# An attention-and-feed-forward kernel: its front in another order, plain v loaded sooner and without a block-diagonal copy

## Chip, cores and metric

The kernel runs on one core of a Trainium2 chip. Times are device microseconds of one execution. Engines are called PE (TensorE, matrix products), DVE (VectorE), ACT (ScalarE), POOL (GpSimd) and SP (SyncE, which here only issues DMAs). POOL, SP and ACT issue DMAs; a load that casts from float32 to float16 on its way is issued by POOL.

## What is computed

The attention of 8 batches with 8 heads of 576 positions and 64 dimensions feeds a gated feed-forward block. Four heads see a plain window of 32 positions, four a dilated one (every fourth of 128). Cut to what matters:

```
mask_plain = (rel >= 0) & (rel < 32)
mask_dil = (rel >= 0) & (rel < 128) & (rel % 4 == 0)
attn = softmax(where(mask, q @ k.T / 8, -1e9))       # heads 0-3 plain, 4-7 dilated
x = (attn @ v).transpose(0, 2, 1, 3).reshape(4608, 512)
out = (gelu(x @ w_gate) * (x @ w_val)) @ w_out       # 512 -> 1536 -> 512
```

## The kernel before

**Tiles.** A unit of attention is a pair of heads of one batch, numbered n: n // 4 is the batch, and for batch 0 n = 0 and 1 are plain pairs and 2 and 3 dilated ones. The results of pair n go to a quarter of x transposed, `xT[pair(n)]`, 128 rows by 4608 tokens. The feed-forward block runs in 9 chunks of 512 tokens. Each chunk has 12 blocks nb of 128 hidden units; a block takes a gate and a value product of four 512-wide matmuls each (line 611, one for each quarter kc of x), then ACT's gelu (g) and DVE's multiply (u). The second product, line 618, follows.

**Words.** The order of the work is written out by hand in strings of words (`gate_words`, `out_words`), one word after another, read by `run_program`. A number counts feed-forward matmuls taken from a list in the order that `orders` gives (block, gate or value, quarter). The others name a unit: c casts loaded q or k to float16, t turns it with PE transposes (t0 to t3 plain, t4 to t7 dilated; q and k of each pair) and copies it out of PSUM, b puts mask biases into PSUM, S makes scores, P the exponential (ACT), D the sums of exponentials, N the product with v, and X (DVE) the division into xT. The reciprocal of a sum comes either from T and B on DVE (two 32x32 transposes and a reciprocal), or from A, which is l and r on ACT (a logarithm and an exponential). W is a filler product on ones; G loads ACT's gelu table; V issues the next loads.

**The front.** Chunk 0 can't start before the attention of batch 0, so the string for c == 0 (lines 802 to 805) does that first: this is "the front". Ahead of it, lines 674 to 698 issue loads and warming products. SP loads q of the plain heads in two halves (line 676), ACT k likewise. `gate["dma"]` holds a DMA that the next gated load must wait for; here the loop leaves the second half of q in it, and the first plain v load (line 235, `load_v(0, 0, True)`, four loads of 144 KB into `stage`) waits for that. POOL issues the dilated q and k (`load_eights`, line 176, four loads), six casting loads of dilated v (lines 301 and 309), then the first two pairs of gate and value weights (`load_w`, line 153), then casts plain v into `vdiag` (`cast_diag`, line 255), then the third pair of weights. [...]

**Plain v of batch 0.** `vdiag` is block-diagonal: the two heads of a pair lie in opposite corners of a 128x128 block, with zeros (line 195, on DVE) in the other two, so that N of a plain pair of batch 0 is 10 full-size matmuls (line 435). All other N units are pairs of 64x64 tiles (line 446), two matmuls for each block.

Of the kernel before, what the change touches and what calls it, by code (L numbers as in the profile page):

```python
# [9 lines left out]
F16 = mybir.dt.float16  # L10
F32 = mybir.dt.float32
# [10 lines left out]
def kernel(  # L22
# [10 lines left out]
    nc = tc.nc  # L33
    B, H, S, D = q.shape
    NT, DM = out.shape
    DFF = moe_w_gate.shape[1]
    P = 128
    NHP = H // 2
# [13 lines left out]
    NB2 = S // BK  # L52
# [5 lines left out]
    const = ctx.enter_context(tc.tile_pool(name="const", bufs=1))  # L58
# [22 lines left out]
    xT = [const.tile([P, NT], F16, tag=f"xT{i}", name=f"xT{i}") for i in range(NKC)]  # L81

    vraw = [const.tile([P, 4 * NB2 * D], F16, tag=f"v{i}", name=f"v{i}") for i in range(3)]
    vdiag = const.tile([P, 2 * NB2 * P], F16, tag="vdiag")
    qraw = [const.tile([P, 2 * QK], F16, tag=f"q{i}", name=f"q{i}") for i in range(2)]
    stage = const.tile([P, 3840], F32, tag="stage")
    s16 = const.tile([P, 4608], F16, tag="s16")
# [52 lines left out]
    def biases():  # L140
        for x in range(2):
            half = slice(64 * x, 64 * x + 64)
            nc.vector.tensor_scalar(bias[half, 0:BQ], band[half, 64 * x : 64 * x + BQ], 1.0, BIG, ALU.subtract, ALU.mult)
        rest = bias[:, BQ : BQ + BK]
        rest_mask(nc.vector, rest)
        nc.vector.tensor_scalar(rest, rest, 1.0, BIG, ALU.subtract, ALU.mult)

    def load_w(*parts):

        for i in parts:  # L150
            for t, w in ((wg_t, moe_w_gate), (wv_t, moe_w_val)):
                src = w[:, WC[i][0] : WC[i][1]].rearrange("(kc p) n -> p kc n", p=P)
                nc.gpsimd.dma_start(out=t[i], in_=src)
# [7 lines left out]
    gate = {}  # L161
# [6 lines left out]
    def rows_in(src, r):  # L168

        return src.rearrange("h (p r) d -> p h (r d)", r=r)  # L170
# [15 lines left out]
    def at2(t, c0, dims):  # L186
        base = t[:, c0 : c0 + 1]
        return bass.AP(tensor=base.tensor, offset=base.offset, ap=[base.ap[0]] + dims)

    diag = vdiag.rearrange("p (e c) -> p e c", c=P)  # L190

    def zero():

        for x in range(2):
            nc.vector.memset(at2(vdiag[64 * x : 64 * x + 64].bitcast(F32), 32 - 32 * x, [[64, 2 * NB2], [1, 32]]), 0.0)

    def st_of(i):
        return stage[:, 1280 * i : 1280 * i + 1280]

# [28 lines left out]
    def load_v(b, i, plain):  # L228

        st = st_of(i)  # L230
        for g in range(2 * plain):
            for x in range(2):
                rows_ = v[b, 2 * g + x].rearrange("(j p) d -> p j d", p=64)
                dst = st[half_of(x, b and g), 576 * g : 576 * g + 576].rearrange("p (j d) -> p j d", j=NB2)
                gated(nc.sync.dma_start(out=dst, in_=rows_))
        for g in range(2 - 2 * plain):
            for x in range(2):
                half = st[half_of(x, g), 576 * g : 576 * g + 512]
                rows_ = v[b, HK + 2 * g + x, 0 : 4 * P].rearrange("(i p r) d -> p i (r d)", i=2, r=4)
                nc.sync.dma_start(out=half.rearrange("p (i c) -> p i c", i=2), in_=rows_)  # L240
        for x in range(2 - 2 * plain):
            dst = st[half_of(x), 512:1152].rearrange("p (g c) -> p g c", c=64)[:, 0:10:9]
            heads = slice(HK + 1, HK + 3) if x else slice(HK, HK + 4, 3)
            nc.sync.dma_start(out=dst, in_=v[b, heads, S - 64 : S].rearrange("g p d -> p g d"))
# [2 lines left out]

        nc.gpsimd.tensor_copy(dst, st_of(i)[:, 0:1152].rearrange("p (e d) -> p e d", d=D))  # L248

    def cast_diag(g):  # L250

        st = st_of(0)[:, 0:1152].rearrange("p (e d) -> p e d", d=D)
        at = slice(NB2 * g, NB2 * g + NB2)
        for x in range(2):
            nc.gpsimd.tensor_copy(diag[half_of(x), at, half_of(x)], st[half_of(x), at])

    def half_of(x, swap=0):
        y = x ^ (1 if swap else 0)
        return slice(64 * y, 64 * y + 64)

    def odd(n):

        return n % 2 if n >= NHP else 0
# [72 lines left out]
    def pair(n):  # L336
        return (n + 2 * (n // NHP in (2, 3))) % NHP

    def is_plain(n):
        return pair(n) < NHP // 2  # L340
# [54 lines left out]
    def win(n, at):  # L395

        bank, kind = at // 10, at % 10
        return 512 * bank + ((0, 832, 960, 0) if is_plain(n) else (80, 880, 880, 64))[kind]
# [13 lines left out]
    def bias_first(n, bank):  # L412

        base = base_of(n, bank)
        tiles["bias", n] = True

        def part(c0, step, k, w, src=None, st=False):
            rhs = at2(bias, BQ if src else 0, [[0, k], [1, w]])
            o = at2(psf, base + c0, [[step, k], [1, w]])
            nc.tensor.matmul(o, ident, rhs, start=st, stop=False, skip_group_check=True)  # L420

        if is_plain(n):
            part(0, BQ, 5, BQ, st=True)
            part(5 * BQ, BQ, 3, BQ, st=True)
            part(8 * BQ, BK, 1, BK)
        else:
            part(0, 176, 3, BQ, st=True)
            part(BQ, 176, 2, 80)
            part(2 * 176 + BQ, 176, 2, 80, st=True)
            part(3 * 176, 176, 1, BQ)  # L430
            part(LD - BK, BK, 1, BK, src=True)

    def emit(mms):
        for o, lhs, rhs, st, end in mms:
            nc.tensor.matmul(o, lhs, rhs, start=st, stop=end, skip_group_check=True)

    def emit_tiles(*lists):

        queues, at = [list(mms) for mms, _ in lists], [0.0] * len(lists)
        while any(queues):  # L440
            i = min((i for i in range(len(lists)) if queues[i]), key=lambda i: at[i])
            o, lhs, rhs, st, end = queues[i].pop(0)
            at[i] += max(int(np.prod(rhs.shape[1:])), 72)
            for x in range(2):
                rows, cols = half_of(x), half_of(x, lists[i][1])
                nc.tensor.matmul(o[cols], lhs[rows], rhs[rows], start=st, stop=end, skip_group_check=True)  # L446
# [91 lines left out]
    def two_num_mms(n, i):  # L538
        b, hp = n // NHP, n % 2
        _, _, _, _, vp, vd = tiles["two", b]  # L540
        tiles["num", n] = win(n, i)
        if is_plain(n):
            vp = vp if b else diag
            return two_mms(n, win(n, i), lambda e: vp[:, NB2 * hp + e, :])
        return two_mms(n, win(n, i), lambda e: vd[:, NB2 * hp + (8 if e is None else e % 2 * 4 + e // 2), :])

# [6 lines left out]

    def two_num(n, i):
        mms = two_num_mms(n, i)
        if n < NHP and is_plain(n):
            emit(mms)
        else:
            emit_tiles((mms, odd(n)))

    def two_t(n):
        dt = nrm.tile([P, 18, 32], F32, tag="dt", bufs=1)
# [93 lines left out]
    def warm(n, bank, rows=P, cols=CH):  # L656

        for _ in range(n):
            nc.tensor.matmul(ps[0:rows, bank, 0:cols], ones[:, 0:rows], ones[:, 0:cols], start=True, stop=True)
# [14 lines left out]
    for h in range(0, HK, 2):  # L674
        for t, src, eng in ((0, q, nc.sync), (1, k, nc.scalar)):
            first = eng.dma_start(out=first_p[:, t, h : h + 2], in_=rows_in(src[0, h : h + 2], 6))
            if t == 0:
                gate["dma"] = first
    load_v(0, 0, True)
    nc.scalar.preload_act_table_set("natural_log_exp_and_others")  # L680
    identity()
# [4 lines left out]
    v_cast(0, 1)  # L686
    tiles["two", 0] = views(0)

    warm(69, 7, 32, 32)
    warm(4, 7)  # L690
    nc.vector.tensor_reduce(class_of, ident.rearrange("p (i r) -> p r i", r=4), axis=mybir.AxisListType.X, op=ALU.max)
    biases()
    zero()
    bias_first(0, 4)
    load_w(0, 1)
    for g in range(2):
        cast_diag(g)
    load_w(2)

    def second():  # L700
# [97 lines left out]
    def gate_words(c):  # L798

        if c == 0:  # L800
            return (
                "c0@0 c1@0 t0@0@1 t1@1@0 b1@6 W1@3@0 S0@4 P0 t4@0@1 W1@3@0 c2@0 c3@0 t5@1@0 t2@2@1 t3@3@0 D0@40 T0 B0 "
                "t6@1@1 W10@7 t7@0@0 S1@6 P1 b2@2 S2@2 P2 D1@60 T1 B1 b3@0 S3@0 P3 D2@20 A2 N0@40 X0 D3@00 N2@60 X2 A3 N3@20 1 "
                "N1@00 X1 X3 G V 15 g0 u0 g1 u1 4 g2 4 g3 4 u2 4 u3 4 g4 4 g5 4 u4 4 u5 4 g6 4 g7 4 u6 4 u7 4 g8 4 g9 4 u8 3 "
                "y0@4@5 y1@6@7 1 u9 8 g10 u10 1 t12@4@1 t14@6@0 t13@5@1 t15@7@0 7 g11 u11"
            )
        loads = {1: "F3", 2: "R", 3: "F5 H5", 4: "F6 H6", 5: "F7 H7"}.get(c, "")
        rest = " ".join(f"4 g{nb} 4 u{nb}" for nb in range(2, NNB - 1))
        if c == 1:
            return f"{loads} 8 G 3 g0 1 u0 3 g1 1 u1 {rest} 4 g{NNB - 1} 4"  # L810
        before = f"e3@{c - 1}" if c < NCH - 1 else ""
        return f"{before} {loads} 7 G 3 g0 1 u0 1 g1 4 u1 {rest} 4 g{NNB - 1} 4" + (f" u{NNB - 1}" if c > 6 else "")

    def out_words(c):
# [15 lines left out]
        )  # L830

    orders = {
        0: "000 100 002 102 010 110 012 112 001 101 011 111 003 103 013 113",
        1: "002 003 012 013 000 010 102 103 112 113 001 011 100 110 101 111",
        2: "002 003 000 102 103 100 012 013 010 001 011 101 112 113 110 111",
        3: "000 001 002 100 101 102 010 011 012 003 013 103 110 111 112 113",
# [39 lines left out]
```

## Time and profile before

| | us |
|---|---|
| three runs | 326.84, 327.86, 326.78; median 326.84 |
| profiled execution | 327.72 |
| its span, first to last instruction | 326.0 |
| PE busy | 320.4 (98%) |
| ACT busy | 159.6 |
| DVE busy | 150.3 |
| POOL busy | 82.2 |
| line 611, gate and value products | 112.5 and 112.3 |
| line 618, output products | 96.3 |

The profile is of one execution. An instruction's line there is a line of the kernel before; the timeline merges neighbours of one kind ("x40") and gives start, length, engine, line, operation, tiles, and in brackets the idle time ahead of it and what ended it. [...] stream of 512-wide products, each shown as about 380 ns, starts one every 216 ns. The span has 1.7 us around it in the profiled execution's own time. TensorE's clock is given as fully granted for the whole execution.

### The profile page before, as it was taken

What the parts mean: (1) busy time and instruction counts of PE and PEld (TensorE: products, weight loads), DVE (VectorE), ACT (ScalarE), POOL (GpSimd) and SP (SyncE); (2) the same over time, 40 slices, a digit from 0 to 9 for tenths busy, and PEclk for the clock granted to TensorE, in tenths of its full rate; (3) what the DMA queues carried; (4) which work ended last, traced back from release to release, by engine and by line L of the source; (5) the groups of instructions that cost most, each with busy time, mean ns of one, the idle gap of its engine ahead of it and who ended that gap; (6) DMA issues with size and microseconds to landing.
All of it is one profiled execution on the core that took longest, in us unless ns stands there. A gap on an engine that the chain in (4) does not pass through costs nothing.

```text
span 326.0 us, 7737 instructions
## 1 busy us (share of the span) xinstructions
PE 320.4 (98%) x3207; PEld 156.5 (48%) x3207; DVE 150.3 (46%) x226; ACT 159.6 (49%) x240; POOL 82.2 (25%) x134
## 2 busy tenths in 40 slices
PE   7999999999999999999999999999999999999996
PEld 5854544444444454445444454445444544444443
DVE  6864636444644464346533654456334644204310
ACT  2662567435753556346633763366435753233321
POOL 8875603402473332241133201411000000000000
DMA  8999997998699997897789527973000200020002
GB/s 190 185 198 206 205 187 154 268 177 197 162 279 166 215 206 212 196 227 176 204 207 226 129 101 161 243 173 103 32 2 1 101 33 0 2 97 32 0 34 97
DMA packets 106659, 47.11 MB, mean 144 GB/s; under 512 B 83584, under 2 KB 102144, under 8 KB 106624
## 3 DMA queue, kind: packets, MB, share of 16 engines
q1 hardware_dynamic: 93120, 38.29, 50.2%
q0 software_dynamic: 12944, 7.67, 16.9%
q10 hardware_dynamic: 560, 0.66, 0.7%
q8 instruction: 25, 0.41, 0.5%
q14 instruction: 10, 0.08, 0.1%
HBM read 37.75 MB, written 9.44 MB: 145 GB/s over the span
## 4 chain that ended last, share of the span: by engine, by line
PE 92%; DMA 2%; POOL 2%; ACT 1%; DVE 1%; issue 0%
PE ps L611 57%; PE ps L618 28%; PE ps L446 6%; DMA wg<-in_moe_w_gate_dram 2%; POOL xT L176 1%; PE ps L642 1%; POOL v L301 1%; ACT P L476 0%; DVE P L481 0%; ACT L793 0%; POOL v L309 0%; PE ps L366 0%; PE ps L386 0%; POOL band L117 0%; ACT g L770 0%
## 5 line engine op out<-in xcount | busy, mean ns | idle before, releaser
L775 DVE SCALAR_TENSOR_TENSOR u_all<-g,ps 128x512 f16<-128x512 f16 x108 | 74.1, 687 | 110.1 <-PE ps L611 93.4
L770 ACT ACTIVATE g<-ps 128x512 f16<-128x512 f32 x108 | 63.6, 597 | 104.0 <-PE ps L611 104.0
L611 PE MATMUL ps<-xT,wg 128*128 128x512 f16 x432 | 112.5, 379 | 0.2 <-DMA wg<-in_moe_w_gate_dram 0.2
L611 PE MATMUL ps<-xT,wv 128*128 128x512 f16 x432 | 112.3, 379 | 0.0
L618 PE MATMUL ps<-wo,u_all 128*128 128x512 f16 x420 | 96.3, 380 | 0.0
L611 PEld LDWEIGHTS <-wv 128*128 128x128 f16 x432 | 42.1, 98 | 51.1 <-DMA wv<-in_moe_w_val_dram 0.6
L611 PEld LDWEIGHTS <-wg 128*128 128x128 f16 x432 | 42.2, 98 | 50.6 <-DMA wg<-in_moe_w_gate_dram 0.3
L618 PEld LDWEIGHTS <-u_all 128*128 128x128 f16 x420 | 39.1, 98 | 45.5 <-issue 0.5
L602 DVE TENSOR_TENSOR xT<-ps,rb 128x576 f16<-128x576 f32 x32 | 28.7, 937 | 16.9 <-PE ps L446 13.6
L476 ACT ACTIVATE P<-ps 128x832 f16<-128x832 f32 (+1 forms) x32 | 25.3, 835 | 16.3 <-PE ps L446 16.2
L211 POOL CAST s<-stage 128x640 f16<-128x640 f32 x24 | 17.1, 742 | 52.5 <-DMA stage<-in_q_dram 35.9
L248 POOL CAST v<-stage 128x1152 f16<-128x1152 f32 x11 | 12.7, 1157 | 62.6 <-DMA stage<-in_v_dram 62.6
L573 ACT ACTIVATE lg<-ps 128x576 f32<-128x576 f32 x30 | 18.7, 653 | 11.6 <-DVE xT L602 8.9
L631 DVE TENSOR_SCALAR osb<-ps 128x512 f32<-128x512 f32 x22 | 15.1, 685 | 12.2 <-PE ps L618 11.8
L579 ACT ACTIVATE rb<-lg 128x576 f32<-128x576 f32 x30 | 19.5, 690 | 0.3
L629 ACT ACTIVATE osb<-ps 128x512 f32<-128x512 f32 x13 | 7.8, 597 | 21.1 <-PE ps L618 21.1
L223 POOL CAST s<-stage 128x512 f16<-128x512 f32 x24 | 14.1, 616 | 10.3 <-DMA stage<-in_q_dram 8.3
L481 DVE TENSOR_TENSOR P<-P,two_p 128x832 f16<-128x832 f16 x14 | 9.7, 693 | 9.8 <-ACT P L476 9.8
L481 DVE TENSOR_TENSOR P<-P,two_d 128x768 f16<-128x768 f16 x14 | 8.8, 633 | 9.6 <-ACT P L476 8.8
L795 ACT ACT_TABLE_LOAD x9 | 11.5, 1283 | 0.2
L446 PEld LDWEIGHTS <-v 64*64 64x64 f16 x616 | 7.7, 107 | 6.3 <-issue 5.9
L446 PEld LDWEIGHTS <-q 64*64 64x64 f16 x576 | 7.9, 107 | 5.1 <-issue 3.2
(67 smaller groups left out, 138.0 us busy)
## 6 DMA issues: line engine op xcount, KB each, us to landing
out_dram<-osb SPq DMA_DIRECT2D x35, 256.0 KB, 2.7
stage<-in_v_dram SPq DMA_DIRECT2D x28, 144.0 KB, 4.0
stage<-in_q_dram SPq DMA_DIRECT2D x24, 128.0 KB, 3.2
stage<-in_k_dram SPq DMA_DIRECT2D x24, 128.0 KB, 3.1
stage<-in_q_dram SPq DMA_DIRECT2D x6, 512.0 KB, 4.7
stage<-in_k_dram SPq DMA_DIRECT2D x6, 512.0 KB, 5.4
stage<-in_v_dram SPq DMA_DIRECT2D x20, 128.0 KB, 2.8
wo<-in_moe_w_out_dram POOLq DMA_DIRECT2D x3, 512.0 KB, 16.4
```

The source lines that it names most:

```text
L211: nc.gpsimd.tensor_copy(s16[:, 1280 * t + 640 * g : 1280 * t + 640 * g + 640].rearrange("p (k c) -> p k c", k=5), st_of(i).rearrange("p (k ...
L446: nc.tensor.matmul(o[cols], lhs[rows], rhs[rows], start=st, stop=end, skip_group_check=True)
L476: nc.scalar.activation(pt[:, 0 : src.shape[1]], src, AF.Exp, bias=0.0, scale=scale)
L481: nc.vector.tensor_tensor(pt, pt, mask, ALU.mult)
L573: nc.scalar.activation(lg, psf[:, c0 : c0 + S], AF.Ln)
L579: nc.scalar.activation(rb, tiles.pop(("lg", n)), AF.Exp, scale=-1.0)
L602: nc.vector.tensor_tensor(dst, num, rb, ALU.mult)
L611: nc.tensor.matmul(ps[:, bank, :], w[:, kc, ns], xT[kc][:, tok], start=first, stop=end)
L618: nc.tensor.matmul(ps[:, bank, :], u_all[:, fc, tb * P : (tb + 1) * P], wo_t[fc // 4][:, fc % 4, :], start=(fc == 0), stop=(fc == NNB - 1),)
L631: nc.vector.tensor_scalar(osb, ps[:, bank, :], 1.0 / USCALE, None, ALU.mult)
L770: nc.scalar.activation(g, ps[:, gate_banks(c, args[0])[0], :], AF.Gelu)
L775: nc.vector.scalar_tensor_tensor(u_all[:, nb, :], tiles.pop(("g", nb)), USCALE, val, ALU.mult, ALU.mult)
```

## The change

It touches the front alone. Unit words keep their meaning.

- `vdiag`, its zeros and its casts go. Plain v of batch 0 is cast to the ordinary v tile, half by half (`cast_first`), and N0 and N1 become pairs of 64x64 tiles.
- On POOL the cast of half 0 follows the first pair of weight loads, the cast of half 1 the second pair.
- The first plain v load waits for the first half of q (`setdefault` keeps the first one) and not for the second.
- 69 warming products of 32 columns become 37 of 32 and 16 of 64. The four of 512 columns stay.
- In the string of chunk 0 the plain turns t2 and t3, the cast c2 and c3 and the scores S1 come ahead of the dilated turns t6 and t7; the fillers after t4 and t6 (one product of 512 columns, ten of 160) go; pair 1 takes l and r on ACT instead of T and B on DVE; N1 comes ahead of D3 and N2; four gate products instead of one stand in front of the last N unit, which is now N3; and the turns y0 and y1 of batch 1 come two products later, behind u9.
- The first 16 feed-forward products go in another order: first the quarters 0 and 1, then 2 and 3.

```
-    vdiag = const.tile([P, 2 * NB2 * P], F16, tag="vdiag")
...
-    def cast_diag(g):
-
-        st = st_of(0)[:, 0:1152].rearrange("p (e d) -> p e d", d=D)
-        at = slice(NB2 * g, NB2 * g + NB2)
-        for x in range(2):
-            nc.gpsimd.tensor_copy(diag[half_of(x), at, half_of(x)], st[half_of(x), at])
+    def cast_first(g):
+
+        nc.gpsimd.tensor_copy(vraw[0][:, 576 * g : 576 * g + 576], st_of(0)[:, 576 * g : 576 * g + 576])
...
-            vp = vp if b else diag
...
-        if n < NHP and is_plain(n):
-            emit(mms)
-        else:
-            emit_tiles((mms, odd(n)))
+        emit_tiles((mms, odd(n)))
...
-                gate["dma"] = first
+                gate.setdefault("dma", first)
...
-    warm(69, 7, 32, 32)
+    warm(37, 7, 32, 32)
+    warm(16, 7, 32, 64)
     warm(4, 7)
...
-    zero()
     bias_first(0, 4)
-    load_w(0, 1)
-    for g in range(2):
-        cast_diag(g)
+    for i in range(2):
+        load_w(i)
+        cast_first(i)
     load_w(2)
...
-                "c0@0 c1@0 t0@0@1 t1@1@0 b1@6 W1@3@0 S0@4 P0 t4@0@1 W1@3@0 c2@0 c3@0 t5@1@0 t2@2@1 t3@3@0 D0@40 T0 B0 "
-                "t6@1@1 W10@7 t7@0@0 S1@6 P1 b2@2 S2@2 P2 D1@60 T1 B1 b3@0 S3@0 P3 D2@20 A2 N0@40 X0 D3@00 N2@60 X2 A3 N3@20 1 "
-                "N1@00 X1 X3 G V 15 g0 u0 g1 u1 4 g2 4 g3 4 u2 4 u3 4 g4 4 g5 4 u4 4 u5 4 g6 4 g7 4 u6 4 u7 4 g8 4 g9 4 u8 3 "
-                "y0@4@5 y1@6@7 1 u9 8 g10 u10 1 t12@4@1 t14@6@0 t13@5@1 t15@7@0 7 g11 u11"
+                "c0@0 c1@0 t0@0@1 t1@1@0 b1@6 W1@3@0 S0@4 P0 c2@0 c3@0 t4@0@1 t2@2@0 t3@3@1 t5@1@0 D0@40 T0 B0 S1@6 P1 b2@2 S2@2 P2 "
+                "t6@0@1 t7@1@0 D1@60 l1 r1 b3@0 D2@20 S3@0 P3 l2 N0@40 X0 r2 N1@60 X1 D3@00 l3 r3 N2@20 X2 4 N3@00 X3 G V 12 g0 u0 g1 u1 4 g2 4 g3 4 u2 4 u3 4 g4 4 g5 4 u4 4 u5 4 g6 4 g7 4 u6 4 u7 4 g8 4 g9 4 u8 4 u9 1 "
+                "y0@4@5 y1@6@7 7 g10 u10 1 t12@4@1 t14@6@0 t13@5@1 t15@7@0 7 g11 u11"
...
-        0: "000 100 002 102 010 110 012 112 001 101 011 111 003 103 013 113",
+        0: "000 001 100 101 010 011 110 111 002 102 012 112 003 103 013 113",
```

## The prediction

> **What bounds the kernel now.** First the chain of waits for the front, then TensorE's timeline, then GpSimd's, then the DMA packets by queue.
>
> ```profile
> 10.18 7.55 DMA wg<-in_moe_w_gate_dram
> 17.72 0.05 issue
> 17.77 0.39 PE ps L611
> 18.16 0.38 PE ps L435 x10
> 18.54 16.91 PE ps L611 x78
> ```
>
> The chain runs through the first gate weights (issued 10.18, landed 17.7) into products that never pause again: 78 in 16.91 us is 216.8 ns each, the pace of a 512-wide product. Section 4 of the page puts 92% of the span on PE. So time before 17.7 can be saved only as far as the dense stream starts earlier, and whatever delays it is paid in full.
>
> ```profile
> 16.46 1.13 PE L446 MATMUL ps<-P,v 64*64 64x96 f16 x40
> 17.77 0.39 PE L611 MATMUL ps<-xT,wg 128*128 128x512 f16 x1 [0.18 <-DMA wg<-in_moe_w_gate_dram]
> 18.00 0.54 PE L435 MATMUL ps<-P,vdiag 128*128 128x96 f16 x10
> 18.44 0.81 PE L611 MATMUL ps<-xT,wg 128*128 128x512 f16 x3
> ```
>
> TensorE waits 0.18 us for the weights, does one product, then N1 (0.44 us), then 15 products; the second block pair starts at 21.69. Sixteen products (16 x 0.216 = 3.46) and N1 end there, so this stretch is worth a gap-free start at 17.79. That is my mark.
>
> ```profile
> 10.18 0.78 POOL L153 DMA_DIRECT2D wg<-in_moe_w_gate_dram  x1
> 11.05 0.74 POOL L153 DMA_DIRECT2D wv<-in_moe_w_val_dram  x1
> 12.71 0.74 POOL L153 DMA_DIRECT2D wg<-in_moe_w_gate_dram  x1 [0.91 <-DMA v<-in_v_dram]
> 13.44 0.75 POOL L153 DMA_DIRECT2D wv<-in_moe_w_val_dram  x1
> 14.17 2.13 POOL L255 CAST vdiag<-stage 64x576 f16<-64x576 f32 x3
> 16.76 0.67 POOL L255 CAST vdiag<-stage 64x576 f16<-64x576 f32 x1 [0.46 <-DMA stage<-in_v_dram]
> 17.37 0.74 POOL L153 DMA_DIRECT2D wg<-in_moe_w_gate_dram  x1
> ```
>
> The last cast waits for plain v (landed 16.7) and frees N1 at 17.43, harmless since N1 stands behind a weight product. In the built program each POOL load waits for the one eight places before it: the first gate weights for the third dilated load (landed 9.95), the first value weights for the fourth (10.8).
>
> ```profile
> q1 hardware_dynamic: 2319, 0.58, 87.2%
> q0 software_dynamic: 846, 0.30, 57.4%
> ```
>
> These are the packets from 9.36 (first of plain v) to 14.3, queue q1 being SP's and q0 POOL's. While both are loaded, 3 v packets pass for one of POOL's. In the same table for 7 to 9 us q0 alone moved 0.39 MB, for 14.5 to 19 us 0.85 MB: 194 and 190 GB/s, its ceiling here.
>
> [...] with q1 present, total GB/s is 182 instead of 194. Plain v moved earlier is therefore moved in front of something. [...] early transposes start every 80 ns, those at 9.7 every 43 ns; [...]
>
> **The change part by part.**
> 1. Warming: 69 products of 32 columns become 37 of 32 and 16 of 64. The former start every 26.7 ns[...]. 69 x 26.7 = 1.84 us; 37 x 26.7 + 16 x 53.3 = 1.84 us. Nothing.
> 2. The two memsets of vdiag (0.54 us each) leave VectorE; the second ended at 5.43, though q's first half landed at 5.0 (0.81 + 4.2). The cast can start 0.4 earlier, but TensorE is busy with the bias products until 5.86 and transposed at 6.08: 0.2 us earlier.
> 3. Fillers W1 and W10 go (0.22 + 0.69 us of TensorE), S1 moves ahead of the last dilated turns. The first scores follow at about 7.9 instead of 8.08, S1 at 10.9 instead of 12.28, S2 at 11.7 instead of 13.2: spare time, since TensorE must then wait for data.
> 4. Plain v is issued when q's first half lands (5.05) and not the second (6.78). Its first packet came 2.6 us after issue (9.36), so now near 7.65. By then about 255 of the 576 KB of dilated loads have moved; 320 KB remain, 1.65 us alone. A 1 KB packet costs 16 engines x 2 us / 381 = 84 ns of an engine; a v packet (16 x 4.94 - 0.30 MB at 190 GB/s x 16) / 2319 = 23 ns. At 3 to 1 a round takes 84 + 70 = 154 ns: 104 KB/us, done at 10.75 instead of 9.4. With the 1.4 us lag of before the last dilated load lands at 12.1 (bounds: 10.8 if it loses nothing, 13.5 if v keeps 6 to 1). V has passed 936 packets by then; the other 1370 at 2319/4.94 = 469 per us end at 13.65 instead of 14.3: it lands 0.65 earlier, near 16.05 (bounds 15.0, if each load keeps its 6.9 to 7.8 us from issue, and 16.7).
> 5. On POOL the order is now first weights, cast of half 0, second weights, cast of half 1, third weights. Queued behind a waiting cast are the second weights, behind the next the third. The first value weights go out at 12.35 (behind 12.1), half 0 lands near 13.9, cast to 14.65 (0.68 us: 576 columns between the 616 ns for 512 and 742 for 640), two issues to 16.15, cast of half 1 to 16.85; with the low bounds 15.8. The third weights leave near 16.9 instead of 17.37; their products need them only at 25.1, and only the value half, landed 26.8 and used at 26.85, was tight.
> 6. First weights: all bytes ahead of them are unchanged and the engines were full, so they land at 17.7 as before, or up to 0.4 sooner, if they trail the last byte by 1.55 us, as the later weights do, and not by 2.0. Issued later, at about 11.4, they still queue.
> 7. N1 now stands ahead of D3, N2 and the weight products, so its cast counts. Cast end + 0.1 + N1 0.45 + D3 0.43 + N2 0.52 gives the start of the stream: 18.35 from 16.85, 17.3 from 15.8, then held at 17.7 by the weights. D3 also needs the last dilated turn: 12.1 + 0.1 + 0.4 (turn) + 1.15 (copies) + 0.2 + 0.5 (scores) + 0.2 + 0.83 (exponential) + 0.2 = 15.7, not the last. N0 and N1 as 20 half-size tiles cost what the 40 at 16.46 do, 0.56 per 20, against 0.44: 0.1 each, inside the terms above. N3 sits in the stream as N1 did.
>
> Sum against the mark 17.79: +0.56 with my middle values, -0.1 with the low ones, and with v at 16.7 and two late issues about +1.2. I take +0.4, between the first two, because four v loads kept 6.9 to 7.8 us from issue whatever queued beside them. From 21.7 on, counts are the same; y0 and y1 go two products later, with both inputs landed (34.8 against 35.4). So the profiled 327.72 us (span 326.0 and 1.7 around it) becomes 328.1; the runs' median of 326.84 becomes 327.2.
>
> **The rivals.**
> (a) *Weights remain the bound.* v lands at its low bound, N1 is free by 16, and only the first gate weights count: 0 to -0.9 us with scatter, point 326.5. For it: the 0.18 us wait names them. Against: POOL's two issues between the casts.
> (b) *The loads really shift.* If v used DMA time idle before, everything behind would land up to 1.7 us earlier (6.78 - 5.05): 325.1. Against: the DMA share is 9 in nearly every slice from 4.5 us on.
> (c) *Slower: the clock falls.* [...] I count 3.5 us of work between 11.7 and 16.9, the longest gap about 1.5, so it is unlikely.
> (d) *The change does not do what it says*: v is issued no earlier, because SP is held. SP's one wait ahead of it was the second half of q, so this is nearly excluded; 326.8.
>
> **How the numbers follow.** Forecast 0.58, (a) 0.28, (b) 0.04, (c) 0.07, (d) 0.03. About 0.5%, 1.6 us, is what a measurement of this kernel tells from no change; the forecast, (a) and (d) lie inside. Faster 0.04, same 0.89, slower 0.07. The range leaves out (b), (c) and the far ends: 325.9 to 328.1.
>
> **What would show it.** Right: q1 packets from 7.6; last dilated load landed near 12; cast of half 1 ending at 16 to 17; N1 waiting for POOL; dense products at 17.8 to 18.6 and the second block pair at 21.7 to 22.4. Wrong: gate weights landing before 17, a dense start before 17.3, or products at 430 ns after 17.

## The result: slower, by a pause that no step had

| | before | after |
|---|---|---|
| median of four runs | 326.96 us | 330.05 us |
| lowest, highest | 326.78, 327.86 | 329.91, 330.21 |
| profiled execution | 327.72 us | 330.21 us |
| its span | 326.0 us | 328.5 us |
| TensorE's granted clock, mean of the span | 1.0 | 0.994 |

The ratio is 1.0089 [1.007, 1.0108]. By the medians the kernel after is 3.1 us slower, by the ratio 2.9; 0.4 was forecast. The profiles of the kernel before and of e1 (below) hold no record of the clock, and 1.0 is what is given then; their dense stream has one product every 217 ns, as the kernel after has where its granted clock is 1.00 (from 21.87 on). In the kernel after, line 596 holds the gate and value products (611 before), 435 all paired 64x64 tiles (scores and N), 424 the sums of exponentials, 409 the biases, 355 the dilated turns, 152 the weight loads, 244 the casts of plain v.

TensorE's timeline of the kernel after, in the front:

```profile
12.48 0.53 PE L424 MATMUL ps<-P,two_ones 128*128 128x384 f16 x5
13.34 0.35 PE L409 MATMUL ps<-bias,ident 128*128 128x288 f16 x2 [0.33 <-ACT q L333]
16.14 0.30 PE L409 MATMUL ps<-bias,ident 128*128 128x160 f16 x3 [2.45 <-issue]
...
17.08 1.26 PE L435 MATMUL ps<-P,v 64*64 64x96 f16 x40
...
19.82 1.57 PE L596 MATMUL ps<-xT,wg 128*128 128x512 f16 x4
21.32 0.54 PE L435 MATMUL ps<-P,v 64*64 64x96 f16 x20
...
24.40 0.81 PE L596 MATMUL ps<-xT,wg 128*128 128x512 f16 x3
```

The second block pair starts at 24.40 and not at 21.69: 2.71 us of loss are made here, about all of the 2.5 between the two spans. The dense stream starts at 19.82 instead of 17.77. And TensorE stops for 2.45 us in the middle of a unit of five bias products, between the second and the third. The bracket says "issue": the profile shows nothing that was waited for. In e1 the third product waits 0.32 us for a copy by VectorE; here that copy was done, since VectorE does nothing between 13.70 and 16.14 (first window below).

The chain of waits of the kernel after runs through that pause and no longer through the weights:

```profile
13.34 0.35 PE ps L409 x2
13.70 2.45 issue
16.14 0.30 PE ps L409 x3
...
19.89 1.50 PE ps L596 x4
21.39 0.47 PE ps L435 x20
21.87 16.73 PE ps L596 x77
```

From 21.87 the stream is as even as before: 77 in 16.73 us, 217 ns each. The other new thing is in the products around 18 to 21: four weight products take 1.57 us there, and 1.04 from 21.80 on, where the clock is 1.00. The windows of the kernel after (stretch, length, busy time of PE, PEld, DVE, ACT and POOL with counts, granted clock, DMA share, GB/s):

```profile
13.70:16.14 2.44, 0.00 (x0) 0.00 (x0) 0.00 (x0) 0.83 (x2) 1.91 (x3) 1.00 1.45 186
14.12:17.53 3.41, 1.39 (x51) 1.33 (x52) 0.00 (x0) 0.69 (x2) 2.73 (x5) 1.00 1.45 193
17.53:20.94 3.41, 3.41 (x57) 2.46 (x50) 2.45 (x3) 3.33 (x6) 3.37 (x6) 0.50 1.38 202
```

After the pause the clock is 0.50 for 3.41 us. So the loss has two parts. With e1 below, whose profile has the same units in the front without the pause and, by the pace of its products, without the half clock, they can be estimated: there the way from the third bias product (14.66) to the stream (19.04) is 4.38, of which 1.46 is a wait, so 2.92 of work. From 16.14 that gives 19.06 at full clock. *Pause:* 19.06 - 17.77 = 1.3. *Half clock:* 24.40 - 19.06 minus the 3.92 from 17.77 to 21.69 = 1.4. Together 2.7. All four runs have a mean clock of 0.994 or 0.995, so the second part stands on this profile alone: no run of this kernel shows it without the half clock. The first part isn't what can be won by taking the pause away: in e1 the stream starts at 19.04 without it, because a wait for plain v stands in its place.

**What the pause goes with.** The profile's list of DMA queues, which the prediction passed over here, has a queue q8, "instruction", with 25 packets of together 0.41 MB in both kernels, 16 KB each, beside the queues that carry the data. In the trace the first of them starts at 13.17 in the kernel after and at 9.73 in the kernel before. Two lines of the table of DMA packets show it (queue and kind, packets, MB, share of the 16 engines). Kernel after, 13.00 to 13.20:

```profile
q8 instruction: 1, 0.02, 46.2%
```

Kernel before, 9.70 to 10.20:

```profile
q8 instruction: 1, 0.02, 17.4%
```

Theory A: the pause belongs to these packets. It comes at a fixed count of TensorE's instructions and ends some 3 us after the start of the first packet (2.97 here), and with fewer instructions ahead of the front that packet starts later. What a packet holds, and what calls for it, the traces don't show. Rival B: the missing fillers are the cause of the half clock, and the pause is a by-product (rival (c) of the prediction). Rival C: v loaded sooner pushes the other loads back, and N1 waits for them (the prediction's own chain, mis-sized). The texts recorded ahead of e1 to e4 call A "theory 1" and B "theory 3"; their "theory 2" is that plain v, issued sooner, holds the instruction packet back.

### The profile page after: what moved, and what is told of

Same layout as the page of the kernel before. It is cut to its first block, busy times and chain, and to the rows that moved or that the text cites. A ratio compares the mean times of both kernels' runs of the same rounds, so it can differ in the third digit from the quotient of the medians.

```text
span 328.5 us, 7718 instructions
## 1 busy us (share of the span) xinstructions
PE 320.7 (98%) x3200; PEld 156.8 (48%) x3200; DVE 149.4 (45%) x221; ACT 160.6 (49%) x242; POOL 81.4 (25%) x132
## 3 DMA queue, kind: packets, MB, share of 16 engines
q0 software_dynamic: 12944, 7.67, 16.7%
## 4 chain that ended last, share of the span: by engine, by line
PE 95%; ACT 2%; DVE 1%; issue 1%
PE ps L596 57%; PE ps L603 27%; PE ps L435 7%; PE ps L644 1%; ACT P L465 1%; PE ps L627 1%; PE ps L409 1%; ACT q L333 0%; DVE P L470 0%; ACT L778 0%; PE ps L355 0%; PE ps L424 0%; PE ps L352 0%; PE ps L375 0%; DVE q L337 0%
## 5 line engine op out<-in xcount | busy, mean ns | idle before, releaser
L558 ACT ACTIVATE lg<-ps 128x576 f32<-128x576 f32 x31 | 19.3, 653 | 11.6 <-DVE xT L587 8.6
L616 DVE TENSOR_SCALAR osb<-ps 128x512 f32<-128x512 f32 x22 | 15.1, 686 | 12.2 <-PE ps L603 11.6
L564 ACT ACTIVATE rb<-lg 128x576 f32<-128x576 f32 x31 | 20.2, 690 | 0.4
L215 POOL CAST s<-stage 128x512 f16<-128x512 f32 x24 | 14.3, 624 | 9.7 <-DMA stage<-in_q_dram 6.7
L470 DVE TENSOR_TENSOR P<-P,two_d 128x768 f16<-128x768 f16 x14 | 9.5, 685 | 9.5 <-ACT P L465 8.8
L435 PEld LDWEIGHTS <-v 64*64 64x64 f16 x656 | 9.3, 110 | 6.7 <-issue 6.0
L780 ACT ACT_TABLE_LOAD x9 | 11.5, 1283 | 0.2
L435 PE MATMUL ps<-P,v 64*64 64x96 f16 (+5 forms) x656 | 11.1, 202 | 0.0
```

The costliest lines, as they stand in the source:

```text
L470: nc.vector.tensor_tensor(pt, pt, mask, ALU.mult)
L558: nc.scalar.activation(lg, psf[:, c0 : c0 + S], AF.Ln)
L564: nc.scalar.activation(rb, tiles.pop(("lg", n)), AF.Exp, scale=-1.0)
L616: nc.vector.tensor_scalar(osb, ps[:, bank, :], 1.0 / USCALE, None, ALU.mult)
```

## The experiments

All kernels compute the whole function; nothing reads what the warming products and fillers, products of ones, write. Ratios are to the kernel before, measured together with each group (medians 327.11 for e1 to e4, 327.36 for e5 to e8, 327.39 for e9 to e12).

**e1: the kernel after with the old 69 warming products**, so 16 more products (32 instructions, as each has its own weight load) and the same columns.

```
-    warm(37, 7, 32, 32)
-    warm(16, 7, 32, 64)
+    warm(69, 7, 32, 32)
```

> The changed kernel with the 69 warming products of 32 columns of before in place of 37 of 32 and 16 of 64: 32 PE instructions more ahead of the front, the same PE time. Theory 1 [...]: the first 16 KB packet on the instruction queue starts at 9.5 to 10.5 us and not at 13.17, no pause over 0.4 us before the dense products, no half clock, second block pair at 21.6 to 22.1, time 326.4 to 327.3. Theory 2 (plain v, moved earlier, holds the instruction packet back on the DMA engines, whatever the count): the packet still starts after 12, a pause of 1 us or more, time 328.5 or more. Theory 3 (the missing fillers let the clock fall, and the pause is only what the trace makes of it): as in the changed kernel, 329.5 to 330.5.

Measured: 328.96, ratio 1.0058 [1.0043, 1.0073]. The packet started at 9.39, close to what theory 1 expects, the pause is gone, and in the profiled execution so is the half clock; the time that theory 1 expected was missed. So the pause of 2.45 us goes with the number of warming products, and 1.2 of the 3.1 us hang on it by the medians (3.09 - 1.85), 1.0 by the ratios. What is left is the chain that the prediction had named. TensorE's timeline of e1, then GpSimd's:

```profile
17.61 0.58 PE L435 MATMUL ps<-P,v 64*64 64x96 f16 x20 [1.46 <-POOL v L244]
...
19.04 1.04 PE L596 MATMUL ps<-xT,wg 128*128 128x512 f16 x4
...
23.08 0.59 PE L596 MATMUL ps<-xT,wg 128*128 128x512 f16 x2
```

```profile
13.46 0.75 POOL L152 DMA_DIRECT2D wv<-in_moe_w_val_dram  x1 [1.76 <-DMA xT<-in_k_dram]
14.26 0.66 POOL L244 CAST v<-stage 128x576 f16<-128x576 f32 x1
...
16.89 0.67 POOL L244 CAST v<-stage 128x576 f16<-128x576 f32 x1 [0.53 <-DMA stage<-in_v_dram]
```

N1 waits 1.46 us for the cast of half 1, and that cast for v itself. Against the kernel before, the stream starts 1.27 later and the second block pair 1.39.

**e2: the kernel after, with plain v behind the second half of q again.**

```
-                gate.setdefault("dma", first)
+                gate["dma"] = first
```

> The changed kernel with plain v issued behind the second half of q again, as before. Theory 1: the instruction packet still starts at 12 to 13.5 and the pause stays at 2 us or more, time 329 to 330.5. Theory 2: the packet starts at 9.5 to 10.5, the pause is gone, time 326.4 to 327.5. Theory 3: 329.5 to 330.5.

Measured: 330.14, ratio 1.0105 [1.0082, 1.0128]: no better. The packet came at 11.5 and the pause shrank to 0.49, but the casts came later (15.26 and 17.35), N0 waited 0.66 us and N1 1.54, and the half clock came all the same (18.22 to 21.63). So the clock fell here with a pause of 0.49 us and waits of 0.66 and 1.54. What the fall costs is not clear from the times: three of the four runs have a mean clock of 0.990 to 0.995 and took 329.97 to 331.33, the fourth has 0.999 and took 330.00.

**e3 and e7: the kernel before with fewer warming products**, 53 (37 of 32 columns, 16 of 64) and 37 (5 and 32), always the same columns.

```
-    warm(69, 7, 32, 32)
+    warm(37, 7, 32, 32)        # e7: 5
+    warm(16, 7, 32, 64)        # e7: 32
```

> The kernel before with only the warming products changed (37 of 32 columns, 16 of 64), fillers and order as before. Theory 1: the instruction packet moves from 9.73 to 12 to 13.5; [...] PE pauses there 1 to 2 us, time 328 to 330. Theory 2 and theory 3: the packet stays near 9.7, no pause, time 326.6 to 327.3.

> The kernel before with 5 warming products of 32 columns and 32 of 64: the same PE time as 69 of 32, 64 PE instructions fewer. Theory A[...]: its first 16 KB packet starts later than the 11.11 of the kernel before with 53 warming products, at 12 to 13.5, and PE pauses for 0.8 to 2 us at 14 to 15; time 327.6 to 329. Theory B: the packet is at 9.7 to 11.2 and nothing changes, 326.8 to 327.4.

Measured: 327.13, ratio 1.0002 [0.9992, 1.0012], and 327.24, ratio 0.9999 [0.9992, 1.0006]. The packet moved from 9.73 to 11.11 and to 12.33, and pauses of 0.52 and 0.44 us appeared. TensorE's timeline of e7:

```profile
15.27 0.49 PE L446 MATMUL ps<-q 64*64 64x96 f16 x16 [0.44 <-issue]
...
17.93 0.39 PE L611 MATMUL ps<-xT,wg 128*128 128x512 f16 x1
```

The stream still starts at 17.93 (17.77 before), and the second block pair at 22.31; the rest of the span makes up for these 0.6 us. Such amounts are made up behind the front now and then (a wait for DVE near 183 us is 0.31 in the profile of before and none in that of e7), so a difference of half a us at the block pair says little. So pauses of 0.52 and 0.44 us left the ratio at 1.000 here; the times that the recorded texts expect with a pause, from 327.6 up, were missed. That the pause of the kernel after costs because it is longer and its front has less spare time is an argument; no run puts 2.45 us into the front of before.

**e4: the kernel before with plain v sooner** (the edit of e2 the other way round).

> The kernel before with only plain v issued behind the first half of q. Theory 1: the packet stays near 9.7, no pause, time 326.3 to 327.4. Theory 2: the packet moves to 12 to 13.5 and PE pauses 1 to 2.5 us near 13.5, time 328 to 330. Theory 3: no pause, 326.3 to 327.4.

Measured: 328.54, ratio 1.0045 [1.003, 1.006], so 1.4 us from this line alone. Its GpSimd, and the N unit that waits for it:

```profile
14.35 0.74 POOL L153 DMA_DIRECT2D wg<-in_moe_w_gate_dram  x1 [1.93 <-DMA v<-in_v_dram]
...
15.82 2.86 POOL L255 CAST vdiag<-stage 64x576 f16<-64x576 f32 x4
```

```profile
17.29 0.55 PE L435 MATMUL ps<-P,vdiag 128*128 128x96 f16 x10 [1.12 <-POOL vdiag L255]
```

A weight load waits 1.93 us for a load of dilated v, and leaves at 14.35; in the kernel before the same weight load waits 0.91 us and leaves at 12.71. All four casts stand behind it. Rival C holds here, and none of the three theories had it. The packet came 1.2 later too (10.93), with a pause of 0.61.

**e5: the kernel after with the ten fillers of 160 columns put back** between the last two dilated turns (`t6@0@1 W10@7 t7@1@0`): rival B by itself.

> The changed kernel with the ten filler products of 160 columns back between t6 and t7 (20 PE instructions, 0.7 us). Theory A [...]: the 16 KB packet starts at 12.5 to 13.5 as before and PE pauses until 15.5 to 16.3, 2 us or more; the clock may or may not fall afterwards: 328.2 to 328.8 if it holds, 329.8 to 330.4 if it falls. Theory B (the missing fillers are the cause): no half clock and no pause, 326.6 to 327.5.

Measured: 331.79, ratio 1.0132 [1.0115, 1.015]. TensorE's timeline of e5:

```profile
12.41 0.87 PE L650 MATMUL ps<-ones 128*128 128x160 f16 x10
13.21 0.41 PE L355 MATMUL ps<-ident,xT 72*64 72x72 f16 x13
15.86 0.23 PE L355 MATMUL ps<-ident,xT 72*64 72x72 f16 x3 [2.24 <-issue]
```

The fillers keep neither the pause away nor the half clock (17.41 to 20.82), and the time is above what either theory expected. And the pause has moved into another unit: with 20 more instructions (ten loads, ten products) ahead of it, it now cuts a run of transposes. Rival B falls as the cause of the pause.

**What all runs say of theory A.** Count the products of TensorE in the trace from the start: wherever such a pause comes in the front, it is ahead of the 224th, whatever work stands there. With one weight load for each, that is the 448th record of weight loads and products.

| kernel | packet starts | 224th product starts | between | pause | the 224th is of |
|---|---|---|---|---|---|
| e9 | 6.68 | 15.31 | 8.63 | none | |
| e11 | 6.75 | 15.08 | 8.33 | none | |
| before | 9.73 | 13.04 | 3.31 | none | |
| e1 | 9.39 | 13.34 | 3.95 | none | |
| e6 | 10.20 | 13.60 | 3.40 | none | |
| e10 | 10.54 | 13.67 | 3.14 | none | |
| e8 | 10.14 | 12.94 | 2.79 | 0.40 | dilated turn |
| e12 | 10.74 | 13.52 | 2.78 | 1.15 | dilated turn |
| e4 | 10.93 | 13.76 | 2.83 | 0.61 | biases |
| e3 | 11.11 | 13.95 | 2.84 | 0.52 | plain scores |
| e2 | 11.50 | 14.21 | 2.71 | 0.49 | biases |
| e7 | 12.33 | 15.27 | 2.94 | 0.44 | plain scores |
| e5 | 12.99 | 15.86 | 2.87 | 2.24 | dilated turn |
| after | 13.17 | 16.14 | 2.97 | 2.45 | biases |

No kernel starts its 224th product sooner than 2.7 us after the packet's start. Where there is a pause, it ends 2.7 to 3.0 us after it; where there is none, 3.1 or more have passed. In e8 a second pause comes, ahead of product 352, which is 128 products, or 256 records, later, and ends 2.27 us after the start of the second packet (17.14 to 19.41). TensorE's timeline of e8, in the middle of one N unit:

```profile
18.26 0.53 PE L435 MATMUL ps<-P,v 64*64 64x96 f16 x18
19.41 0.22 PE L435 MATMUL ps<-P,v 64*64 64x64 f16 x2 [0.61 <-issue]
```

The rest of the traces says the same. In all fourteen, TensorE has 16 gaps over 0.1 us that are put down to "issue": nine ahead of product 224 or 352, seven ahead of product 608 (another 512 records on, near 43 us, at most 0.46 long, 0.13 in the kernel before), and none anywhere else. These seven end 2.3 to 2.6 us after the start of the fourth packet. All 16 follow the count, whatever unit stands there. As far as it speaks of counts and times, theory A stands; why the count and the packet go together is not shown. The margin of the kernel before at product 224 was 3.31 - 2.8 = 0.5 us, an estimate from the table.

**e6: e1 with N1 late again**, in the order and the places of the kernel before, and the first 16 feed-forward products in the order of before too. **e8: e6 with v behind the second half of q.** The edit of the string:

```
-  ... l2 N0@40 X0 r2 N1@60 X1 D3@00 l3 r3 N2@20 X2 4 N3@00 X3 G V 12 ...
+  ... l2 r2 N0@40 X0 D3@00 N2@60 X2 l3 r3 N3@20 1 N1@00 X1 X3 G V 15 ...
```

> The changed kernel with 69 warming products of 32 columns, and N1 back behind D3, N2, N3 and one weight product, with the PSUM places and the first 16 products in the order of before; plain v still issued sooner. Theory A (what the kernel with 69 warming products still loses, N1 waiting for the cast of half 1 with D3, N2 and the stream behind it, is the place of N1): the dense stream starts by 17.7 to 18.0, second block pair at 21.7 to 22.1, time 326.8 to 327.5. Rival (v issued sooner makes everything late, and the place of N1 is nothing): second block pair at 22.8 or later, 328.4 to 329.2.

> As the run with N1 late, and plain v issued behind the second half of q as before. What is left of the change is the order of the turns, no block-diagonal v, no fillers. Theory A: no pause over 0.5 us, 326.5 to 327.2. Rival (v issued sooner helps, since the cast of half 0 needs it): later than the run with N1 late and v sooner, 327.8 to 328.8.

Measured: 329.34, ratio 1.0061 [1.0042, 1.008], and 328.52, ratio 1.0029 [1.0018, 1.004]. In e6 the second block pair comes sooner (22.56 against 23.08 in e1), but the third value weights are what then comes last. Its timeline:

```profile
28.90 0.82 PE L596 MATMUL ps<-xT,wv 128*128 128x512 f16 x3 [0.62 <-DMA wv<-in_moe_w_val_dram]
```

They were issued at 18.90, behind the two casts on GpSimd. So N1's place isn't the whole remainder. e8 was the best version with the new front, about 1 us above the kernel before, where 326.5 to 327.2 was expected; its second block pair came at 22.81, with N0 waiting 0.70 for its cast and the two pauses above. No run takes these three apart.

**e10: e2 with fillers in its two waits** (`W8@7` ahead of N0, `W20@7` ahead of N1).

> The changed kernel with plain v behind the second half of q (the run whose clock fell at 18.22, 330.14 us), with 8 filler products of 160 columns ahead of N0 and 20 ahead of N1, where PE waits for the casts anyway. Theory A [...]: no half clock, 328.2 to 328.9. Rival (the clock falls whatever PE does there, or costs nothing): half clock again, or 329.7 to 330.5.

Measured: 329.21, ratio 1.0047 [1.0029, 1.0065], 0.9 less than e2. All four runs have a mean clock of 0.999 or 1.0; in e2 three of four have 0.990 to 0.995. So more work in TensorE's idle time went with a clock that held; the packet came sooner as well (10.54) and its pause was gone, so the fillers needn't have done it alone. The second block pair comes at 22.82 instead of 25.04, but half of these 2.2 us are lost again by the end of the span (327.4 against 328.5): what is lost at the block pair is not all in the time.

**e9 and e11: 101 products of 32 columns and 2 of 512** (in place of 69 and 4, the same columns), in the kernel after and in the kernel before, to bring the packet earlier still.

> The changed kernel with 101 warming products of 32 columns and 2 of 512 in place of 37, 16 of 64 and 4 of 512: 92 PE instructions more, the same columns as with 69. Theory A [...]: the first 16 KB packet starts by 9 us, before the 9.39 to 10.2 seen with 69; no pause, no half clock; what stays is the wait for the casts and loads, so second block pair at 22.3 to 23.3 and 328.0 to 329.2. Rival [...]: 9.4 or later.

> The kernel before with 101 warming products of 32 columns and 2 of 512, the same columns as its own. Theory A: the packet starts before its 9.73, by 1 us or more; no pause was there to be removed, so the time stays, 326.8 to 327.6, unless the dilated loads are held back by the packet, then up to 328.

Measured: 329.19, ratio 1.0051 [1.0027, 1.0075], and 330.42, ratio 1.0062 [1.0027, 1.0097]. The 330.42 is the median of eleven runs from 327.1 to 332.7; the ratio leaves out the three longest. For e11 326.8 to 328 was expected. The packet came at 6.68 and 6.75, no pause followed; but in both the first dilated turn started at 10.21 instead of 8.57, after waits of 2.12 and 1.81 us for its load, and the clock fell (at 9.58 and 11.53). In e11 the time goes with the mean clock of each run: 327.1 to 328.9 at 1.0, 330.3 and 330.4 at 0.995 and 0.994, 331.7 and 331.8 at 0.988 and 0.989. More instructions ahead of the front aren't simply better.

**e12: e1 with the casts of plain v on DVE**, each right ahead of its N unit.

> The changed kernel with 69 warming products of 32 columns (328.96 us), the two casts of plain v done by DVE ahead of N0 and N1 instead of by POOL between its weight loads. If POOL's order is what that kernel still loses: N1 at 16.8 or earlier, the wait for the third value weights gone, 327.0 to 328.0. If the landing of v and of the last dilated load is: N1 at 17.3 to 17.7 as there, second block pair at 22.7 to 23.1, only the 0.45 us wait for the third value weights gone, 328.3 to 328.8.

Measured: 329.98, ratio 1.0102 [1.0047, 1.0157]. Its timeline:

```profile
17.55 0.58 PE L435 MATMUL ps<-P,v 64*64 64x96 f16 x20 [1.22 <-DVE v L244]
```

N1 starts at 17.55, as in e1 (17.61): GpSimd's order isn't what holds it. v landed at 16.54 here and at 16.76 in e1, so its landing is what both wait for first; between it and N1 lie the cast (0.45 us here) and some 0.5 us more. The time was above the expected 328.3 to 328.8, with runs from 329.2 to 332.9.

## Why the prediction was wrong

*Step 1, "Warming ... Nothing", is the one that failed.* It counted columns, which were indeed the same: all warming products take 3.84 us in both kernels, 73 before and 57 after. It should have counted instructions: in the kernel before the packet moves by 1.2 to 1.5 us for each 16 products (6.75, 9.73, 11.11, 12.33 for 101, 69, 53, 37), and in the kernel after from 9.39 (e1) to 13.17. The 224th product also lies 16 products further into the front with 16 warming products less. The profile showed q8; nothing that the prediction read of it showed that it mattered. What step 1 put at nothing went with a pause of 2.45 us and a half clock of 3.41 us behind it, 1.2 of the 3.1 us by the medians of e1. Of the 1.85 us that e1 still loses, 1.27 are there when its stream starts, behind the late v (step 4).

*Step 3* took the fillers that go, and the earlier scores, as spare time. The first part stood (e5). Whether the earlier scores were spare, no run shows by itself.

*Step 4* had the packets right in the profile of after: v issued at 4.91 (5.05 foreseen), its first packet 7.45 (7.65), the last dilated packet 10.8 (10.75), the last dilated load landed at 11.6 (12.1). It had the landing of v wrong, and so the wait of N1. It let v end at 14.3 in the kernel before, but there 42 packets of SP's queue came after 14.5, the last at 15.7; that the last of after came at 13.68, where 13.65 was foreseen, is luck. v landed at 14.8 in the kernel after and at 16.8 in e1, with 16.05 foreseen and bounds of 15.0 and 16.7. The sum leant on four v loads that kept 6.9 to 7.8 us from issue; in e1 the last two took 9.6, so that v, issued 1.8 us sooner than in the kernel before (4.98 against 6.78), landed no sooner (16.76 against 16.71).

The traces show which part came late. The landing of each of these loads is recorded as 16 increments of a semaphore:

| kernel | first instruction packet | load | 15th increment | 16th |
|---|---|---|---|---|
| before | 9.73 to 11.12 | last of v | 15.26 | 16.71 |
| e1 | 9.39 to 10.98 | last of v | 15.32 | 16.76 |
| e4 | 10.93 to 12.28 | last of v | 14.60 | 16.22 |
| after | 13.17 to 14.65 | last of v | 14.67 | 14.77 |
| e9 | 6.68 to 7.94 | first dilated | 8.49 | 10.16 |
| e11 | 6.75 to 7.97 | first dilated | 8.43 | 10.17 |

For loads of plain v and of dilated q and k that landed before that packet started, the 16th increment comes at most 0.6 us after the 15th, in all twelve kernels that have such loads. For the last v load it comes 0.65 to 2.5 us after it in thirteen of the fourteen, and 0.1 in the kernel after, whose packet came last of all. So one increment in 16 is the late one: by 1.67 us for the first dilated load of e9 (packet at 6.68), by 1.45 us for v in the kernel before (9.73), and by only 0.10 us in the kernel after (13.17), which has the pause of 2.45 us instead. What holds the late part up is not shown.

*Step 5* foresaw the cast of half 1 ending at 16.85. GpSimd's timeline of the kernel after:

```profile
10.63 0.78 POOL L152 DMA_DIRECT2D wg<-in_moe_w_gate_dram  x1 [0.47 <-DMA xT<-in_q_dram]
11.93 0.75 POOL L152 DMA_DIRECT2D wv<-in_moe_w_val_dram  x1 [0.52 <-DMA xT<-in_k_dram]
12.84 0.66 POOL L244 CAST v<-stage 128x576 f16<-128x576 f32 x1 [0.17 <-DMA stage<-in_v_dram]
...
14.93 0.68 POOL L244 CAST v<-stage 128x576 f16<-128x576 f32 x1
```

The first gate weights wait for the third dilated load and the first value weights for the fourth, as foreseen. Casts and loads start in the order of the program: in e1 the cast of half 1 waits 0.53 us, starts at 16.89, and the third weights leave behind it at 17.50. The cast ends at 15.6, below even the low bound. In e1 it is the other way: the cast ends at 17.56, above the middle value. *Step 6* was right: the first gate weights landed at 17.63 (17.72 before).

*Step 7* had the right chain, and e1 shows it: cast end to stream 19.04 - 17.56 = 1.48, foreseen 1.5. The term that was mis-sized is v's landing, 0.7 later than foreseen, so that the front loses 1.3 us and not 0.56. e1, the kernel after without the pause, is 1.85 us slower than the kernel before, outside the range too. In the profile of after itself N1 doesn't wait for GpSimd: the pause covers it.

*Rivals.* (a) and (b) fell: the stream starts 2 us later. (d) fell: v was issued sooner, and the front's order is as written. (c) had the right side, and the half clock came, for 3.41 us and, by the profile, an estimated 1.4 of loss. That it was unlikely was the author's estimate: no trace of the kernel before shows a fall. That it always costs so much isn't shown: two of the four runs of e1 had a mean clock of 0.995 and took 328.84 and 329.07, the two at 1.0 took 328.42 and 329.23. But the missing fillers were not the cause (e5: with them back, half clock from 17.41 to 20.82), and "the longest gap about 1.5" was too low by about 0.95, since the gap was the pause of 2.45, which no count of work could show.

*Open.* What sets the packet's start. The number of products ahead of the front moves it in the same direction in both kernels, at four counts in the one and three in the other; plain v sooner goes with a later packet in two pairs (9.73 to 10.93 from before to e4, 11.50 to 13.17 from e2 to after) but not from e8 (10.14) to e6 (10.20). Kernels that are the same up to there scatter by 1.4 us (e1 9.39, e6 10.20, e12 10.74), so a single step of that size is no proof. Counted from the record 256 ahead of the pause, the 192nd, the packet comes 4.4 and 4.8 us later in e5 and in the kernel after, in all others 1.6 to 3.2. No run moved the packet alone. How the 1.2 us between the kernel after and e1 divide between the pause and the half clock is open too: two runs of e1 had a mean clock of 0.995 as well, and stayed 0.8 us or more below every run of the kernel after. No version tried beat the kernel before; e3 and e7 equal it.

## What to carry to other kernels

Count instructions as well as work: here 16 tiny products fewer at the start, with the same columns, went with an instruction packet 1.2 to 1.5 us later in the kernel before, and with a pause of 2.45 us in the front of the kernel after. When a timeline shows "issue" in the middle of a unit that waits for nothing, look for the instruction queue's packets some 3 us earlier (2.7 to 3.0 in the front here), and count whether the pause sits at the same instruction in another variant. Before a load is moved ahead of others on DMA engines as full as here (186 to 202 GB/s in the windows of the kernel after), list what each later load releases: one line cost 1.4 us by itself (e4). And compare when a load is issued with when it lands: in e1 v was issued 1.8 us sooner and landed no sooner.

## What the runs showed of the hardware beyond that

**Instruction packets and pauses.** The packets of q8 have 16 KB each. With 186 GB/s moved in the window of the pause, the pause of the kernel after ends 2.97 us after the start of its packet; in all eight kernels that have one in the front it is 2.7 to 3.0 us, and 2.3 to 2.6 us for later pauses. The three places where TensorE stopped are 256 and 512 weight loads and products apart. The first packet takes 1.2 to 1.6 us (13.17 to 14.65 in the kernel after). From its end to the end of the pause it is 1.4 to 1.5 us in all eight kernels that have one.

**The clock fell after stretches less than half busy.** The granted clock fell to 0.50 in five kernels (after, e2, e5, e9, e11). In the 3.41 us ahead of the fall, as long as the half clock in the kernel after, TensorE was busy 1.21 to 1.64 us (1.39 in the kernel after, above); the longest pauses or waits in or into those stretches are 2.45, 1.54, 2.24, 2.12 and 1.81 us. Windows of e2, then of e9:

```profile
14.81:18.22 3.41, 1.21 (x47) 0.98 (x46) 0.76 (x1) 2.03 (x3) 2.96 (x5) 1.00 1.21 154
18.22:21.63 3.41, 3.41 (x49) 2.37 (x48) 1.79 (x2) 1.85 (x3) 3.41 (x6) 0.50 1.25 157
```

```profile
6.17:9.58 3.41, 1.64 (x33) 1.08 (x30) 1.86 (x3) 1.50 (x2) 2.62 (x5) 1.00 1.26 195
9.58:16.41 6.83, 6.20 (x114) 5.21 (x116) 3.46 (x6) 2.74 (x4) 4.91 (x8) 0.50 1.43 187
```

That is 35% and 48% busy. One stretch earlier TensorE was busy 2.66 of 3.41 us in the kernel after and 2.59 in e2, and the clock stayed at 1.00. The half clock lasts 3.41 us in e2 and in the kernel after and 6.83, twice that, in e9. Five falls are no rule, and what sets the fall these runs don't show. The prediction looked for the longest gap alone; in e2 no gap there was longer than 1.54 us, and the clock fell.
